# A list scheduler's model of TensorE's program loading, and the ranks of a dozen groups of work, are changed

## The chip, the cores and the metric

The kernel runs on one core of a Trainium2 chip. The metric is the device time of one execution in microseconds; the median over repeated executions counts. A profiled execution has its own time, and a span, which is the time from its first to its last instruction.

TensorE (PE) multiplies matrices, VectorE (DVE) and ScalarE (ACT) do elementwise work, SyncE (SP) and GpSimd (POOL) mostly issue transfers (DMAs).

## The reference

Two branches work on 2048 tokens of 512 channels each, and a gate per token mixes them:

```python
def _A_ref(u, ...):                       # L = 2048, D = 512, N = 128
    A = -jnp.exp(log_A_real) + 1j * A_imag
    C = (C_real + 1j * C_imag) * dt[:, None]
    P = jnp.exp((A * dt[:, None])[:, :, None] * pos[None, None, :])
    K = 2.0 * jnp.einsum("dn,dnl->dl", C, P).real
    y = irfft(rfft(u_t, 2 * L) * rfft(K, 2 * L))[:, :, :L]
    return y + u * D_skip
def _B_ref(x, w_gate, w_up, w_down):      # F = 1792
    h = einsum("bsd,df->bsf", x, w_gate) * einsum("bsd,df->bsf", x, w_up)
    return einsum("bsf,fd->bsd", h, w_down)

g = sigmoid((x * gate_w).sum(-1))
return g * a + (1 - g) * b
```

Branch B is a bilinear feed-forward layer. Branch A is a long convolution whose kernel K is made from 128 complex modes per channel, and which is done by Fourier transforms.

## The kernel before, in words

**Branch B** is most of TensorE's work. Every float32 operand is split into a high part (`hi`, rounded to the type that TensorE multiplies in one pass) and a rest (`lo`), and a product is three matmuls of 128x512: hi with lo, lo with hi, hi with hi. `pg` and `pu` are the gate and up products (operands `whi`, `wlo`, `xs`), `h` their elementwise product, which DVE makes and ACT and DVE split into `hh` and `hl`, and `y` the down product (`dhi`, `dlo`). The 1792 hidden columns are worked off in four groups of tiles, and for each group the 2048 tokens in four chunks. Finished `y` tiles are scaled into `acc` and added to the output in memory by transfers that accumulate, issued by POOL.

**Branch A** puts smaller work between these products, all of it into the PSUM tile `k`, called *sets* here: a set is a run of small matmuls that belong to one step. There are sets for the first transform of u (`k<-in,w2s` at the start), for the convolution kernel from the tables `x` and `v`, which DVE and ACT build for 32 channels at a time (`k<-v,x`), for the kernel's transform (`k<-kt,w1k_t`), the second transform (`k<-in,w2s` later on), the inverse one (`k<-y,w3s`) and the last one (`k<-in,w_t`). The `k<-v,x` and the `k<-y,w3s` sets are the dense ones: a listing of the program shows 64 matmuls for each, but every float32 matmul is run as two, so the trace shows 128, in about 2 us. Results between transforms go through memory (`su_d`, `sk_d`, `y_d`).

**The order** of all this is not written out. Every piece of work is handed to `Work.add` (line 242) as a task with its engine, an assumed duration in us, the tiles that it reads and writes, and a rank. `Work.plan` (line 340) is a list scheduler. It simulates all engines and the transfers with assumed costs, picks again and again the task that can start first (ties by rank, then by the task's number), and so fixes the order of every engine's instructions when the program is built; on the chip each engine runs its instructions in that order and waits on semaphores where it must. Three parts of this model matter here:

- `Bus` (line 170) stands for the transfers. It keeps two queues, one for those that POOL issues and one for all others, and says when each ends.
- `fetched` (line 314) stands for the loading of PE's own program. The model takes the program to come in blocks of 256 instructions, the loading of a block to be asked for `LEAD` instructions ahead of a point one block before it is needed, and to take `FETCH` us. A PE task that would run past the end of what has been loaded is planned to start later; another that can start sooner is then picked in its place.
- `EASE` (line 219) is a table of small corrections. It names groups of tasks by engine, tiles and assumed duration, and gives each a slack (it counts as ready so many us later) and a change of rank.

Of the kernel before, what the change touches and what calls it, by code (L numbers as in the profile page):

```python
# [115 lines left out]
class InOrder:  # L116


    def __init__(self, tc, engine):
        self.tc, self.engine, self.last = tc, engine, None  # L120
# [49 lines left out]
class Bus:  # L170
# [1 line left out]
    WEIGHT = 1.0, 1.58  # L172

    def __init__(self):
        self.now, self.queues = 0.0, ([], [])

    def serve(self, queues, now, until):
        done = []
# [8 lines left out]
                        done.append((q.pop(0)[0], now))  # L187
        return done

    def add(self, task, at, us):  # L190
        at = max(at, self.now)
        self.serve(self.queues, self.now, at)
        self.now = at
        self.queues[task.engine == "pool"].append([task, us])
        return self.serve([[[*x] for x in q] for q in self.queues], at, 1e9)


class Work:
# [12 lines left out]
    OVERLAP = {"act": 0.09, "dve": 0.08}  # L211


    BLOCK, FIRST, LEAD, FETCH = 256, 193, 25, 6.5
    TABLE = 1.3
    ROOM = {"dve": 0.6, "act": 0.4}
    BEYOND = 60

    EASE = {
        "act:k/in:0.32": (0.0, 1),  # L220
        "act:t/rt:0.77": (0.0, -1),
        "dve:k/kt:0.42": (0.0, -1),
        "dve:t/e/ri:0.85": (0.0, 2),
        "pool:ts:0.95": (2, 0),
        "sp:in:0.42": (0.0, 1),
    }
    DMA_RATE = 0.33

# [10 lines left out]
    def memory(self):  # L239
        return Tile(self, None, None, None, None, None, False)  # L240

    def add(self, engine, us, fn, r=(), w=(), rank=1, after=0.0, dma=0, hold=(), rows=(), count=0, slack=0.0, table=None, urgent=False):


        task = Task(len(self.tasks), engine, us, fn, rank, after, dma)
        task.rows, task.count, task.slack, task.table, task.urgent = rows, count, slack, table, urgent
        self.tasks.append(task)
        clash = lambda p, q: p is None or q is None or p == q
        split = lambda x: x if isinstance(x, tuple) else (x, None)
        for tile, part in map(split, r):  # L250
            task.deps.update(t for p, t in tile.writers if clash(p, part))
        for tile, part in map(split, w):
            task.deps.update(t for p, t in tile.writers + tile.readers if clash(p, part))
        for tile, part in map(split, r):
            tile.readers.append((part, task))
        for tile, part in map(split, w):
            tile.writers.append((part, task))
        for tile, _ in map(split, [*r, *w, *hold]):
            if tile.pool and tile not in task.tiles:
                task.tiles.append(tile)  # L260
                tile.users.append(task)
        task.deps.discard(task)
        return task
# [47 lines left out]
                return True  # L311
        return False

    def fetched(self, task, start, past):

        if not task.count:
            return start
        n0, times = past[-1][0] if past else 0, past
        n1 = n0 + task.count
        step = task.us / task.count  # L320
        first = -(-(n0 - self.FIRST) // self.BLOCK)
        b = self.FIRST + self.BLOCK * max(first, 1)
        while b < n1 + (self.BEYOND if step < 0.05 else 0):
            asked = self.passed(past, b - self.BLOCK - self.LEAD, n0, start, step)
            at = step * (b - n0) if b <= n1 else task.us + 0.11 * (b - n1)
            if asked < start:
                start = max(start, asked + self.FETCH - at)
            b += self.BLOCK
        return start

# [9 lines left out]
    def plan(self):  # L340
        for t in self.tasks:
            tags = "/".join(dict.fromkeys(tile.tag for tile in t.tiles))
            slack, rank = self.EASE.get(f"{t.engine}:{tags[:24]}:{t.us:.4g}", (0.0, 0))
            t.slack, t.rank = t.slack + slack, t.rank + rank
        left = len(self.tasks)
        free = {t.engine: 0.0 for t in self.tasks}
        order, known, rows, past, loaded = [], {}, {}, [], "exp"
        bus, then, users, need = Bus(), {}, {}, {}
        for t in self.tasks:
            need[t] = len(t.deps)  # L350
            for d in t.deps:
                users.setdefault(d, []).append(t)
                if d.dma:
                    then.setdefault(d, []).append(t)
        ready = [t for t in self.tasks if not need[t]]
        while left:
            best, wanted, found, soon = None, {}, [], {}
            for t in ready:
                at = known.get(t)
                if at is None:  # L360
                    at = known[t] = self.inputs(t)
                place = self.slots(t, at)
                found.append((t, place))
                if place is not None:
                    if t.urgent:
                        soon[t.engine] = min(place, soon.get(t.engine, 1e9))
                loose = [x for x in t.tiles if x.loose and x.made is None]
                if loose and not self.kept_waiting(t):
                    for tile in loose:
                        wanted.setdefault(tile.key, []).append((t.rank, at))  # L370
            for t, at in found:
                if at is None:
                    continue
                start = max(at, free[t.engine])
                if best and start > best[0][0]:
                    continue
                if t.rows:
                    start = max([start] + [rows[r] for r in t.rows if r in rows])
                if t.count:
                    start = self.fetched(t, start, past)  # L380
                if any(
                    rank < t.rank and when <= start
                    for tile in t.tiles if tile.made is None and tile.loose for rank, when in wanted.get(tile.key, ())
                ):
                    continue
                if not t.urgent and start < soon.get(t.engine, 0.0) < start + t.us - self.ROOM.get(t.engine, 9.0):
                    continue
                key = (start, t.rank, t.n)
                if best is None or key < best[0]:
                    best = (key, t)  # L390
            assert best, "no work can start"
            (start, _, _), t = best
            ready.remove(t)
            left -= 1
            for x in users.get(t, ()):
                need[x] -= 1
                if not need[x]:
                    ready.append(x)
            if t.count:
                past.append(((past[-1][0] if past else 0) + t.count, start, t.us, t.count))  # L400
            if t.table:
                t.us += self.TABLE * (t.table != loaded)
                loaded = t.table
            t.start, t.end = start, start + t.us
            free[t.engine] = t.end - self.OVERLAP.get(t.engine, 0.0)
            if t.dma:
                for d, end in bus.add(t, start + self.SENT[t.engine], t.dma / self.DMA_RATE / 1000):
                    d.end = end + self.LANDED[d.engine]
                    for x in then.get(d, ()):
                        known.pop(x, None)  # L410
            rows.update((r, t.end) for r in t.rows)
            for tile in t.tiles:
                if tile.made is None:
                    tile.made = start
                    tile.had.append(tile)
            order.append(t)
        return order
# [7 lines left out]
def gated_mix_kernel(  # L425
# [74 lines left out]
    def power_sets():  # L500
        for k in range(NP):
            pool_q.memset(turns[:, k : k + 1], float(TURNS[k]))

    add("dve", 0.5, memsets, w=[m_const, m_skip], rank=0)
    add("pool", 4.0, power_sets, w=[m_powers], rank=0)


    raws = {}

    def load(key, src, rank=0):  # L510
        if key in raws:
            return
        t = raws[key] = new("glu", "raw", [P, D], bufs=2)
        add("sp", 0.42, lambda: sp.dma_start(t.t, src), w=[t], dma=256, rank=rank)
# [1031 lines left out]
```

## Time and profile before

| | us |
|---|---|
| three executions | 589.75, 591.22, 588.7 (median 589.75) |
| profiled execution | 588.13 |
| its span | 586.0 |
| PE busy in it | 574.0 |
| DVE busy in it | 511.6 |
| ACT busy in it | 400.4 |
| POOL busy in it | 113.0 |

A matmul in these profiles is shown from its start to a modelled end, and the next one starts before that, so the busy time of a group is more than what it occupies; how long a run of matmuls takes is read from starts. "PEld" is the loading of a matmul's stationary operand. In a list of waits, "issue" stands for time in which an engine was idle and waited for nothing that the profile shows. The granted clock of TensorE is given as a share of full speed.

### The profile page before, as it was taken

The numbers are of one execution on the slowest core, as the hardware profiler recorded it, in microseconds if no ns is written. First come the engines' busy times: TensorE is split into PE (matmuls) and PEld (weight loads), VectorE is DVE, ScalarE is ACT, GpSimd is POOL, SyncE is SP. The second block draws the span as 40 slices with busy tenths as digits, with TensorE's granted clock in tenths as the row PEclk, the third lists the DMA queues.
The fourth block names the chain that finished last, engine by engine and source line by source line (L and its number), as shares of the span: only waits on it lengthen the run. The fifth ranks groups of instructions, "written<-read, shape, count | busy, mean of one in ns | idle before, by whom it ended". The sixth has DMA issues, their size and how long they took to land.

```text
span 586.0 us, 14846 instructions
## 1 busy us (share of the span) xinstructions
PE 574.0 (98%) x5996; PEld 434.1 (74%) x5996; DVE 511.6 (87%) x812; ACT 400.4 (68%) x891; POOL 113.0 (19%) x159
## 2 busy tenths in 40 slices
PE   8999999999999999989999999999999999999995
PEld 5777777888886767868767878876877788677763
DVE  6999999979999999996999999994999997346845
ACT  5459888897578599837897684799858743333341
POOL 0003222312010241210222301122321003112011
PEclk9999999999999999998999999999999999999998
DMA  8999969998475898987879958889968377799687
GB/s 279 400 354 365 391 223 342 274 228 262 86 190 126 282 239 177 218 231 236 178 246 237 232 152 273 196 206 206 249 181 244 89 231 138 257 333 226 204 182 138
DMA packets 71687, 136.28 MB, mean 233 GB/s; under 512 B 6852, under 2 KB 35780, under 8 KB 69188
## 3 DMA queue, kind: packets, MB, share of 16 engines
q1 hardware_dynamic: 47668, 87.10, 43.4%
q0 software_dynamic: 23392, 47.98, 39.5%
q8 instruction: 47, 0.77, 0.6%
q10 hardware_dynamic: 560, 0.26, 0.2%
q14 instruction: 20, 0.16, 0.1%
HBM read 80.27 MB, written 55.05 MB: 231 GB/s over the span
## 4 chain that ended last, share of the span: by engine, by line
PE 94%; DMA 3%; DVE 1%; issue 1%; ACT 0%; DVEq 0%; SPq 0%; ACTq 0%
PE y L124 26%; PE pg L124 26%; PE pu L124 25%; PE k L124 16%; DMA kt<-in_wts 2%; DMA ev<-in_wts 1%; DVE y L124 0%; DVE hl L124 0%; ACT dhi L124 0%; DVE h L124 0%; DVE x L124 0%; DVE dlo L124 0%; ACT h L124 0%; ACT hh L124 0%; DVE kt L124 0%
## 5 line engine op out<-in xcount | busy, mean ns | idle before, releaser
L124 PE MATMUL pg<-xs,whi 128*128 128x512 f32 x448 | 139.4, 392 | 0.4 <-ACT whi L124 0.4
L124 PE MATMUL pu<-xs,whi 128*128 128x512 f32 x448 | 138.7, 391 | 0.0
L124 PEld LDWEIGHTS pg<-xs,whi 128*128 128x128 f32 x448 | 84.5, 189 | 19.2 <-ACT whi L124 1.9
L124 PEld LDWEIGHTS pu<-xs,whi 128*128 128x128 f32 x448 | 84.6, 189 | 17.1
L124 PE MATMUL y<-dhi,hl 128*128 128x512 f32 x224 | 89.7, 400 | 1.0 <-DVE hl L124 1.0
L124 PE MATMUL pg<-xs,wlo 128*128 128x512 f32 x224 | 90.2, 403 | 0.1
L124 PE MATMUL pu<-xs,wlo 128*128 128x512 f32 x224 | 90.0, 402 | 0.0
L124 PE MATMUL y<-dlo,hh 128*128 128x512 f32 x224 | 87.4, 390 | 0.0
L124 PE MATMUL y<-dhi,hh 128*128 128x512 f32 x224 | 87.3, 390 | 0.0
L124 POOL DMA_DIRECT2D out<-acc x44 | 38.5, 968 | 178.0 <-ACT acc L124 153.3
L124 ACT COPY ev<-k 128x512 f32<-128x512 f32 x112 | 59.1, 597 | 17.1 <-PE k L124 17.0
L124 ACT CAST hh<-h 128x512 fp32r<-128x512 f32 x56 | 34.7, 619 | 43.4 <-DVE h L124 42.9
L124 ACT ACTIVATE acc<-y,ngate 128x512 f32<-128x512 f32 x62 | 41.9, 685 | 28.7 <-PE y L124 26.5
L124 DVE TENSOR_TENSOR h<-pu,h 128x512 f32<-128x512 f32 x56 | 38.5, 687 | 24.3 <-PE pu L124 23.1
L124 PEld LDWEIGHTS pg<-xs,wlo 128*128 128x128 f32 x224 | 42.2, 188 | 21.1 <-issue 11.1
L124 PEld LDWEIGHTS y<-dhi,hl 128*128 128x128 f32 x224 | 42.0, 188 | 20.2 <-issue 8.1
L124 PEld LDWEIGHTS pu<-xs,wlo 128*128 128x128 f32 x224 | 42.3, 189 | 17.9 <-issue 8.9
L124 ACT COPY h<-pg 128x512 f32<-128x512 f32 x56 | 32.8, 586 | 26.9 <-PE pg L124 21.2
L124 PEld LDWEIGHTS y<-dhi,hh 128*128 128x128 f32 x224 | 42.1, 188 | 9.0
L124 PEld LDWEIGHTS y<-dlo,hh 128*128 128x128 f32 x224 | 42.1, 188 | 8.0
L124 DVE TENSOR_TENSOR hl<-h,hh 128x512 fp32r<-128x512 f32 x56 | 38.4, 686 | 3.1 <-ACT hh L124 2.7
L124 DVE TENSOR_TENSOR x<-m,x 128x896 f32<-128x896 f32 x32 | 34.5, 1085 | 0.0
(130 smaller groups left out, 959.2 us busy)
## 6 DMA issues: line engine op xcount, KB each, us to landing
xs<-xs_d SPq DMA_DIRECT2D x36, 512.0 KB, 6.4
out<-acc POOLq DMA_DIRECT2D x44, 256.0 KB, 5.5
raw<-in_wts SPq DMA_DIRECT2D x33, 256.0 KB, 4.5
xs_d<-xs SPq DMA_DIRECT2D x16, 512.0 KB, 7.3
su_d<-ev POOLq DMA_DIRECT2D x32, 256.0 KB, 6.5
y_d<-ts SPq DMA_DIRECT2D x28, 256.0 KB, 5.9
in<-su_d POOLq DMA_DIRECT2D x12, 512.0 KB, 6.9
sk_d<-ev SPq DMA_DIRECT2D x6, 1024.0 KB, 5.8
```

The source lines that it names most:

```text
L124: got = getattr(self.engine, name)(*args, **kw)
```

## The change

In the model of the transfers, `Bus` now keeps a record of how many us of transfers were queued at each moment (`load`). In the model of program loading, the block is taken to be asked for 64 instead of 25 instructions ahead of the point, and to take 5.0 us, plus 1.05 us for each us of transfers queued 1.2 us after the asking (5 us of them at most), in place of a flat 6.5 us. So the model lets PE run a dense set across the end of a block sooner than before where little is queued (5.0 us), and later where much is (up to 10.25 us).

In `EASE`, twelve entries stand where six stood, and each has a third number, which moves the task in the tie-break by so many places. The groups are, in this order: two ACT copies out of `k` (the last quarter's kernel transform, with a slack of 3 us, and the last transform), the copy of C into `x`, the cast of weights into `whi`, the absolute value in the phases, a small DVE fix-up on the second transform (slack 3), the DVE sums into `kt`, the DVE products in the table `v`, the accumulating output of `ts`, the loads of `in` on SP, the store of `ri`, and the load of three constants at the start. The entry of the DVE products into `ri` is gone. The rest of the diff saves time while the program is built (`sign`, `place`, `seen`) and changes nothing in the order.

```diff
@@ class Bus
-        self.now, self.queues = 0.0, ([], [])
+        self.now, self.queues, self.loads = 0.0, ([], []), [(0.0, 0.0)]
...
+    def load(self, at):
+        for then, us in reversed(self.loads):
+            if then <= at:
+                return max(0.0, us - at + then)
+        return 0.0
+
     def add(self, task, at, us):
...
         self.queues[task.engine == "pool"].append([task, us])
+        self.loads.append((at, sum(x[1] for q in self.queues for x in q)))
@@ class Work
-    BLOCK, FIRST, LEAD, FETCH = 256, 193, 25, 6.5
+    BLOCK, FIRST, LEAD, FETCH = 256, 193, 64, 5.0
...
+    BEHIND = 1.05
...
-        "act:t/rt:0.77": (0.0, -1),
+        "act:t/rt:0.77": (0.0, 0, -200),
...
@@ def fetched
             if asked < start:
-                start = max(start, asked + self.FETCH - at)
+                late = self.FETCH + self.BEHIND * min(bus.load(asked + 1.2), 5.0)
+                start = max(start, asked + late - at)
@@ def plan
-            slack, rank = self.EASE.get(f"{t.engine}:{tags[:24]}:{t.us:.4g}", (0.0, 0))
-            t.slack, t.rank = t.slack + slack, t.rank + rank
+            slack, rank, late = self.EASE.get(f"{t.engine}:{tags[:24]}:{t.us:.4g}", (0.0, 0, 0))
+            t.slack, t.rank, t.late = t.slack + slack, t.rank + rank, t.late + late
...
-                key = (start, t.rank, t.n)
+                key = (start, t.rank, t.n + t.late)
```

The built programs hold the same instructions of TensorE in another order: the same 62 sets between the same products. The first place that the prediction speaks of lies at 250 to 263 us of the profile before. Between a `k<-v,x` set and the `k<-y,w3s` set after it PE had nine gate and up products:

```order
L124 MATMUL k<-v,x 32x64 x64
L124 MATMUL pg<-xs,wlo 128x512
L124 MATMUL pg<-xs,whi 128x512 x2
...
L124 MATMUL k<-y,w3s 64x128 x64
```

Now the `k<-v,x` set stands eight products later, and between the two there are eight gate and up products and three down products (33 matmuls where 27 stood):

```order
L124 MATMUL k<-v,x 32x64 x64
L124 MATMUL pg<-xs,wlo 128x512
L124 MATMUL pg<-xs,whi 128x512 x2
...
L124 MATMUL y<-dhi,hl 128x512
L124 MATMUL y<-dlo,hh 128x512
L124 MATMUL y<-dhi,hh 128x512
L124 MATMUL k<-y,w3s 64x128 x64
```

What moved is the pair of dense sets against the products around it: the first one later in the program, the second further behind it.

On SP at about the same place the loads of the next chunk's tokens (`xs`) and the stores of the inverse transform (`y_d`) stand in another order; here the difference, with what stood before marked by a minus:

```order
 L124 DMA in<-y_d 64x2048 x2
+L124 DMA xs<-xs_d 128x1024 x4
 L124 DMA w3s<-in_w 128x512 x2
-L124 DMA y_d<-ts 64x8x128 x2
-L124 DMA xs<-xs_d 128x1024
-L124 DMA y_d<-ts 64x8x128
-L124 DMA xs<-xs_d 128x1024 x2
-L124 DMA y_d<-ts 64x8x128
-L124 DMA xs<-xs_d 128x1024
+L124 DMA y_d<-ts 64x8x128 x4
```

Four loads of `xs` now go ahead of the constants `w3s` and of all four stores of `y_d`.

The last place lies at about 460 us. A `k<-v,x` set, a `k<-y,w3s` set and a `k<-in,w2s` set, which stood as `k<-y,w3s`, `k<-in,w2s`, `k<-v,x`, now follow each other with four products between each two; the first half of it on PE:

```order
L124 MATMUL k<-v,x 32x64 x64
L124 MATMUL pg<-xs,wlo 128x512
L124 MATMUL pg<-xs,whi 128x512 x2
L124 MATMUL pg<-xs,wlo 128x512
L124 MATMUL pg<-xs,whi 128x512 x2
L124 MATMUL pg<-xs,wlo 128x512
L124 MATMUL pg<-xs,whi 128x512 x2
L124 MATMUL pg<-xs,wlo 128x512
L124 MATMUL pg<-xs,whi 128x512 x2
L124 MATMUL k<-y,w3s 64x128 x64
```

The inverse transform's set has moved from ahead of the `k<-v,x` set to behind it, with twelve matmuls between.

More of the change, by code (lines that the diff above doesn't have):

```diff
@@ L217 @@
     BEYOND = 60
+    BEHIND = 1.05
     EASE = {
-        "act:k/in:0.32": (0.0, 1),
-        "act:t/rt:0.77": (0.0, -1),
[L222 to L225, printed above, removed]
+        "act:k/e:0.4": (3, 0, 0),
+        "act:k/in:0.32": (0.0, 1, 0),
+        "act:pb/x:0.31": (0.0, 0, -60),
+        "act:raw/whi:0.62": (0.0, 0, -60),
+        "act:t/rt:0.77": (0.0, 0, -200),
+        "dve:ev/y:0.6": (3, 0, 0),
+        "dve:k/kt:0.42": (0.0, -1, 0),
+        "dve:m/v:1.09": (0.0, 0, -20),
+        "pool:ts:0.95": (2, 0, 0),
+        "sp:in:0.42": (0.0, 1, 0),
+        "sp:ri:0.42": (2, 0, 0),
+        "sp:w3s/w2s/v:1.3": (0.0, 1, 0),
     }
@@ L240, in memory, with add @@
         return Tile(self, None, None, None, None, None, False)
-    def add(self, engine, us, fn, r=(), w=(), rank=1, after=0.0, dma=0, hold=(), rows=(), count=0, slack=0.0, table=None, urgent=False):
+    def add(self, engine, us, fn, r=(), w=(), rank=1, after=0.0, dma=0, hold=(), rows=(), count=0, slack=0.0, table=None, urgent=False, late=0):
         task = Task(len(self.tasks), engine, us, fn, rank, after, dma)
-        task.rows, task.count, task.slack, task.table, task.urgent = rows, count, slack, table, urgent
+        task.rows, task.count, task.slack, task.table, task.urgent, task.late = rows, count, slack, table, urgent, late
         self.tasks.append(task)
@@ L312, in kept_waiting, with fetched @@
         return False
-    def fetched(self, task, start, past):
+    def fetched(self, task, start, past, bus):
         if not task.count:
@@ L354, in plan @@
                     then.setdefault(d, []).append(t)
+            t.keys = {tile.key for tile in t.tiles}
+            t.sign = t.place = None
+        seen = {k: 0 for t in self.tasks for k in t.keys}
         ready = [t for t in self.tasks if not need[t]]
@@ L361, in plan @@
                     at = known[t] = self.inputs(t)
-                place = self.slots(t, at)
+                sign = at, sum(seen[k] for k in t.keys)
+                if t.sign != sign:
+                    t.sign, t.place = sign, self.slots(t, at)
+                place = t.place
                 found.append((t, place))
@@ L379, in plan @@
                 if t.count:
-                    start = self.fetched(t, start, past)
+                    start = self.fetched(t, start, past, bus)
                 if any(
@@ L410, in plan @@
                         known.pop(x, None)
+                    for tile in d.tiles:
+                        seen[tile.key] += 1
+            for tile in t.tiles:
+                seen[tile.key] += 1
             rows.update((r, t.end) for r in t.rows)
```

## The prediction, made before the changed kernel was run

> **What bounds the kernel now.** I read the page first, then who waited for whom on PE, then the chain of waits around the longest wait, then busy time and clock by stretch. From the page:
>
> ```profile
> span 586.0 us, 14846 instructions
> PE 574.0 (98%) x5996; PEld 434.1 (74%) x5996; DVE 511.6 (87%) x812; ACT 400.4 (68%) x891; POOL 113.0 (19%) x159
> q8 instruction: 47, 0.77, 0.6%
> ```
>
> PE is busy for 98% of the span. The third line is the queue that brings program code to PE: 47 packets, 0.77 MB, so 16.4 KB each. PE runs 5996 matmuls and as many loads, 11992 instructions, 255 for each packet: one packet is one block of the planner's 256.
>
> The list of waits, PE's rows, longest first (total, times, longest):
>
> ```profile
> PE k L124 <- issue: 2.8, 1, 2.8
> PE k L124 <- DVE acc L124: 1.5, 1, 1.5
> PE y L124 <- DVE hl L124: 1.0, 1, 1.0
> PE pg L124 <- ACT whi L124: 0.4, 1, 0.4
> ```
>
> In 586 us PE waits four times. Three of these are in the first 27 us. The longest one names no engine; this is its place in the timeline and in the chain of waits:
>
> ```profile
> 249.94 2.00 PE L124 MATMUL k<-v,x 128*32 128x64 f32 x128
> 258.21 1.98 PE L124 MATMUL k<-y,w3s 32*64 32x128 f32 x117
> 263.00 0.46 PE L124 MATMUL k<-y,w3s 32*64 32x128 f32 x11 [2.81 <-issue]
> ```
>
> PE stops inside a set, after 117 of its 128 matmuls, where no operand can be new. Busy time by stretch from the start (PE and PEld with counts), and the code queue's row in two windows, 0 to 260.1 us and 260.6 to 261.6 us:
>
> ```profile
> 0.00:260.10 260.10, 257.20 (x2374) 196.23 (x2374) 246.38 (x410) 198.82 (x438) 51.57 (x95) 1.00 0.87 260
> q8 instruction: 17, 0.28, 0.4%
> q8 instruction: 1, 0.02, 5.9%
> ```
>
> By then PE had run 4748 instructions, and some 50 semaphore instructions that the columns leave out (an estimate, from the program's count of 125 for all). 17 packets hold 4352, so about 448 were there from the start, and the 18th packet passes while PE stands still. So instruction 448 + 256 n needs the packet after n of them. Counted so in the listed order, this crossing falls on matmul 118 of the set; the timeline breaks between 117 and 118. The wait is for code.
>
> **The price of this wait** is more than its 2.81 us:
>
> ```profile
> 263.00:268.00 5.00, 5.00 (x24) 3.89 (x25) 2.78 (x3) 3.48 (x7) 0.00 (x0) 0.66 0.49 139
> 268.00:273.00 5.00, 5.00 (x23) 4.10 (x23) 2.72 (x5) 2.92 (x5) 0.00 (x0) 1.00 0.86 253
> 25.60:26.50 0.90, 0.00 (x1) 0.00 (x0) 0.90 (x4) 0.00 (x0) 0.00 (x0) 1.00 1.00 410
> 26.50:32.00 5.50, 5.44 (x24) 4.52 (x25) 5.46 (x12) 3.35 (x7) 0.00 (x0) 1.00 1.01 325
> ```
>
> The number before the last two is the granted clock: 0.66 for the 5 us after the wait, 5.00 x 0.34 = 1.7 us lost; the chain's rows bear it out:
>
> ```profile
> 254.88 2.72 PE pu L124 x12
> 263.46 3.18 PE pg L124 x9
> 266.64 3.44 PE pu L124 x12
> ```
>
> Twelve matmuls took 2.72 us before (0.227 each) and 3.44 after. 9 and 12 at 0.227 are 4.8 us, they took 6.6, and some 0.2 to 0.3 of that is the usual step out of a set. I take 1.6: the wait costs 2.8 + 1.6 = **4.4 us**. The 1.0 us wait at 25.6 us, last two of the four rows, left the clock at 1.00: a short wait costs itself alone. [...]
>
> **The change part by part.** *It removes and adds no work*: the listed order has the same 62 sets and the same products, 5996 matmuls. At 0.227 us a matmul and 0.2 for each way out of a set, PE's own time is the same. What can change is the four waits, the tail, and new waits.
>
> *The wait at 260 us.* The model now asks 39 instructions earlier and adds queued transfers. In the new order the `k<-v,x` set comes eight products later and 33 matmuls follow it, not 27; the crossing falls on matmul 88 of the `k<-y,w3s` set. From the first set's start to the crossing it was 10.1 us (249.94 to 260.1) and is 1.92 + 0.2 + 33 x 0.227 + 0.1 + 87/128 x 2.03 = 11.1. The code came 263.0 - 249.94 = 13.1 us after the first set's start. If it kept that distance, a wait of 2.0 us would remain. But in the new order PE enters the block before (one block, 256 instructions, ahead of the crossing) only at the end of the `k<-v,x` set, about 5.5 us later against the transfers that held the packet up, which are gone by then. I take 0 left, 2.0 as the other end.
>
> *New crossings.* The order puts four crossings into the second of two close sets, each with the entry into the block before inside the first: 5.5, 5.4, 4.7 and 5.2 us from entry to crossing (at about 220, 330, 462 and 468 us). For the third: entry at matmul 50 of `k<-v,x`, crossing at 38 of `k<-y,w3s`: 78/128 x 1.92 + 0.2 + 12 x 0.227 + 37/128 x 2.03 = 4.7. The nearest case before, from the timeline, and the code queue in 446.7 to 447.8 us, and the other queue in 444 to 446.7:
>
> ```profile
> 444.04 2.00 PE L124 MATMUL k<-v,x 128*32 128x64 f32 x128
> 449.59 1.14 PE L124 MATMUL k<-in,w2s 32*32 32x512 f32 x32
> 450.66 0.50 PE L124 MATMUL y<-dhi,hl 128*128 128x512 f32 x1
> q8 instruction: 1, 0.02, 5.8%
> q1 hardware_dynamic: 295, 1.06, 96.3%
> ```
>
> Entry at matmul 48 of the first, 444.76, crossing at the last matmul of the second, 450.6: 5.9 us, passed without a wait. The packet was through by 447.8, 3.0 us after the entry, though the other queue had been full till 446.7. From a packet's end to running code took 263.0 - 261.6 = 1.4 us, so the code was there 4.4 us after the entry. The four new ones have 4.7 to 5.5: they pass, by 0.3 to 1.1 us, if the packet is as quick as here. If it were as late as at 260 us (entry, in PE's sequencer some 35 instructions ahead, at about 252; code at 263: 11 us), each would cost 5.5 to 6.3 us and the clock. I take the value near the first, since the planner puts them where little is queued: 0.3 us for all four, 0 and 6 as ends.
>
> *The cover of DVE.* The twelve `EASE` entries permute DVE's and ACT's work. Rows: DVE's longest wait in 263 to 300 us, and two stretches (DVE is the third number with a count behind it, after PE and PEld):
>
> ```profile
> DVE h L124 <- PE pu L124: 4.4, 1, 4.4
> 300.00:350.00 50.00, 50.00 (x685) 37.79 (x683) 48.51 (x70) 39.05 (x96) 13.13 (x14) 1.00 0.87 219
> 350.00:400.00 50.00, 50.00 (x604) 39.96 (x600) 49.45 (x72) 38.71 (x93) 9.53 (x10) 1.00 0.88 216
> ```
>
> DVE lost 4.4 us because PE was late, so without the wait both move up together. But DVE is at 98.0 of 100 us from 300 to 400: the cover is 2 us. The reordered sums and table products are the same instructions; I cost them 0, at most 2.4 us (4.4 - 2.0) if DVE is what holds PE after that.
>
> *Start and tail.* Two loads of `dhi` go ahead of three constants, and DVE's order up to 25 us shifts by one or two instructions. The wait for `hl` stays, since the work just ahead of it is the same: 0, within 0.5. At the end:
>
> ```profile
> 573.31 6.37 PE y L124 x27
> 579.70 0.48 DVE kt L124
> ```
>
> PE ends at 579.7 and 6.3 us of DVE and output transfers follow, with the same last instructions: 0, within 0.5.
>
> *Sum.* -4.4 + 0.3 = -4.1 us in the profiled execution: span 581.9 from 586.0, and 584.0 from 588.13, of which 2.1 lie outside the span. The median is 1.6 above the profiled time, and I take the difference over: 589.75 - 4.1 = **585.6 us**.
>
> **The rivals.**
>
> *The wait moves.* Two of the four short crossings come 1 to 1.5 us late each, without loss of clock: -4.4 + 2.5 = -1.9, 587.9. For it: 0.3 us to spare at the tightest. Against: 444 us passed with a full queue.
>
> *The wait stays where it was.* Only 1.0 of 2.8 us is gained there and the clock may still fall: 589.75 - 1.0 = 588.8, or 587.1 with full clock. For it: four `xs` loads follow there sooner than they did. Against: the later entry.
>
> *DVE holds PE* from 300 us: 589.75 - 2.0 = 587.8. For it 98.0 of 100; against: PE waits for DVE nowhere past 27 us.
>
> *The wait isn't one for a packet that could be earlier*, and the order leaves it as it is: PE holds blocks far ahead, something else stops it, 589.75. Against: packet 18 lies in the idle time. [...]
>
> *Slower.* The two crossings at 462 and 468 us come one behind the other, about where POOL issues a transfer of 512 KB (the rows are from the timeline and from the list of issues, with its 6.2 us to landing):
>
> ```profile
> 473.19 0.93 POOL L124 DMA_DIRECT2D x<-su_d  x1 [18.24 <-PE k L124]
> x<-su_d POOLq DMA_DIRECT2D x2, 512.0 KB, 6.2
> ```
>
> If the packets meet it as the one at 252 us met its transfers, both crossings wait over 2.8 us and lose the clock: 2 x 4.4 - 4.4 = +4.4, 594.2. It decides (592.7) from packets that end about 5.2 us after the entry instead of 3.0: two waits of 2 us, each with 1.6 us of clock. Against: at 444 us a full queue did not do that.
>
> **How the numbers follow.** Forecast 0.50 (584.3 to 586.7); the wait moves 0.22; stays 0.09; DVE 0.06; no effect 0.05; slower 0.08. Half a percent, about what a measurement of this kernel tells from no change, is 2.9 us: 586.8 and 592.7. The forecast, and with short lateness a quarter of the second and third cases (0.08), lie below: faster 0.58. Slower 0.08. The rest, 0.34, is the same. The range 583.8 to 590.3 leaves out the slower case, the far end of the second, and a gain larger than one wait, which the executions 588.7 to 591.2 allow if they hold more than one.
>
> **What would show it.** Right: PE has no wait for "issue" over 0.5 us, the granted clock is 1.00 from 263 us to the end, PE still ends 6.3 us before the span does, span 581.4 to 582.6. Wrong: an idle time in a set at about 257 us (stays), at 220, 330 or 460 to 470 us (moves), or `k` and `y` waiting for DVE after 300 us. If the span falls by 2.8 us and the clock still dips, the clock's price was taken wrongly.

## The result, and the profile after

The changed kernel takes 585.71 us in the median of 14 runs (584.38 to 589.44), the kernel before 589.61 in 14 runs beside it (586.63 to 591.66): a ratio of 0.9944, with an interval from 0.9924 to 0.9964. It is 3.9 us faster, and 585.6 was forecast. The profiled execution was the slowest of the 14, 589.44 us, with a span of 587.5, so its profile shows where time went and not the gain; a second profile of the same kernel (`again`, below) has 583.2. Three executions among all the runs told of here were far slower than the rest (811, 948 and 3238 us) and stand in no figure.

From the page of the changed kernel, and its list of waits, PE's rows (total, times, longest):

```profile
span 587.5 us, 14848 instructions
PE 576.0 (98%) x5996; PEld 435.4 (74%) x5996; DVE 511.7 (87%) x812; ACT 399.1 (68%) x891; POOL 113.3 (19%) x159
```

```profile
PE k L124 <- issue: 1.8, 1, 1.8
PE k L124 <- DVE acc L124: 1.5, 1, 1.5
PE k L124 <- DMA in<-sk_d: 1.2, 1, 1.2
PE y L124 <- DVE hl L124: 0.6, 1, 0.6
PE pg L124 <- ACT whi L124: 0.5, 1, 0.5
```

The longest wait is again "issue", but shorter and elsewhere. The timeline shows it in a `k<-v,x` set at 130.6 us, and the set at the old place in one piece:

```profile
128.62 1.98 PE L124 MATMUL k<-v,x 128*32 128x64 f32 x125
132.36 0.30 PE L124 MATMUL k<-v,x 128*32 128x64 f32 x3 [1.76 <-issue]
...
260.92 1.99 PE L124 MATMUL k<-v,x 128*32 128x64 f32 x128
...
270.54 2.10 PE L124 MATMUL k<-y,w3s 32*64 32x128 f32 x128
```

Busy time by stretch, for the two stretches behind the new wait and the two in which DVE was the cover (the granted clock is the number before the last two):

```profile
131.00:136.00 5.00, 3.64 (x13) 2.88 (x14) 3.26 (x5) 3.38 (x10) 0.00 (x0) 0.77 0.60 124
136.00:141.00 5.00, 5.00 (x21) 4.02 (x21) 3.76 (x5) 2.86 (x5) 0.85 (x1) 0.89 0.33 93
300.00:350.00 50.00, 48.84 (x671) 36.91 (x649) 47.17 (x71) 37.96 (x94) 13.96 (x14) 1.00 0.84 205
350.00:400.00 50.00, 50.00 (x626) 39.19 (x626) 49.34 (x73) 37.34 (x92) 9.57 (x10) 1.00 0.92 238
```

The clock's price is there too: 5.00 x (0.23 + 0.11) = 1.7 us. PE lost the 1.16 us between 300 and 350 us to the one wait for `in<-sk_d`, which the kernel before had not. No wait of PE's after the first 29 us was ended by DVE.

Why was this execution 1.5 us longer than the profiled one of before, when the kernel is faster? The same 5 us near the start, the kernel before first and the changed kernel second:

```profile
5.00:10.00 5.00, 4.62 (x19) 3.39 (x19) 4.56 (x14) 3.61 (x9) 0.00 (x0) 1.00 1.06 357
```

```profile
5.00:10.00 5.00, 4.49 (x11) 3.40 (x11) 4.45 (x14) 3.48 (x8) 0.00 (x0) 1.00 1.04 340
```

PE ran 19 matmuls there in the one and 11 in the other, in the same order. (The clock column says 1.00 in both; the clock's record in the trace begins only at 5.1 us in the one and at 10.8 in the other. From one start to the next a wide matmul took 0.43 us up to 10.6 us in the changed kernel, and 0.23 from 6.7 us on in the kernel before.) The first product with `hl` started at 22.72 and 24.88 us: 2.2 us that belong to the execution and not to the kernel, as the next section shows. The rest, all in us, is -2.8 and -1.7 at 260 us, +1.8 and +1.7 at 131, +1.2 for `in<-sk_d`, -0.4 of the wait for `hl`, -0.4 after PE's end (6.0 us against 6.3): +1.6 with the 2.2, and 1.5 is measured.

### The profile page after: what moved, and what is told of

Same layout as the page of the kernel before. It is cut to its first block, busy times and chain, and to the rows that moved or that the text cites. A ratio compares the mean times of both kernels' runs of the same rounds, so it can differ in the third digit from the quotient of the medians.

```text
span 587.5 us, 14848 instructions
## 1 busy us (share of the span) xinstructions
PE 576.0 (98%) x5996; PEld 435.4 (74%) x5996; DVE 511.7 (87%) x812; ACT 399.1 (68%) x891; POOL 113.3 (19%) x159
## 4 chain that ended last, share of the span: by engine, by line
PE 91%; issue 4%; DMA 2%; POOL 1%; ACT 1%; DVE 1%; DVEq 0%; POOLq 0%; ACTq 0%
PE pg L124 26%; PE pu L124 26%; PE y L124 24%; PE k L124 15%; DMA in<-sk_d 1%; DMA y<-in_xT 1%; DMA sk_d<-ev 1%; POOL out L124 1%; POOL in L124 0%; ACT ev L124 0%; DVE y L124 0%; ACT h L124 0%; ACT xs L124 0%; DVE hl L124 0%; DVE dlo L124 0%
## 5 line engine op out<-in xcount | busy, mean ns | idle before, releaser
L124 PE MATMUL pu<-xs,whi 128*128 128x512 f32 x448 | 140.3, 395 | 0.0
L124 PEld LDWEIGHTS k<-v,x 128*32 128x32 f32 x2048 | 29.4, 110 | 7.6 <-issue 7.2
```

The source lines that it names most:

```text
L124: got = getattr(self.engine, name)(*args, **kw)
```

## The experiments

### Both kernels again

The two kernels unchanged, in the order before, changed.

> The kernel before, profiled a second time. Theory A (each execution has a code packet that comes late by chance, at a crossing that differs from run to run): PE again has one or two waits for issue inside a set, 1.5 to 4 us in all, but not surely at 260 us, and the break falls on the matmul that the count 448 + 256 n gives; the time against itself is within 0.5%. Rival (the wait at 260 us belongs to this order): a wait of 2.5 to 3.1 us after matmul 117 or 118 of the same set, and nowhere else.

> The changed kernel, profiled a second time. Its first profile has a span of 587.5 us with a wait for code of 1.8 us at 130.6 us and one of 1.2 us for a transfer. Theory A (late packets by chance): the second profile has at most one wait for code, not at the same place, and a span of 582.5 to 585. Rival (the wait at 130.6 us belongs to the new order): it is there again with 1.5 to 2 us, span 585 to 588. Ratio to the kernel before 0.992 to 0.997 either way.

The kernel before took 590.2 us, a ratio to the other runs of the same kernel of 1.0019 (1.0002 to 1.0035), which says what such a ratio is worth. The changed one took 585.01, ratio 0.9939 (0.9915 to 0.9963). In the second profile of before PE stopped in the same set after the same 117 matmuls, for 3.1 us, and the clock fell again; its first `hl` product came at 24.49 us, so the late start is no mark of the change. In the second profile of the changed kernel:

```profile
span 583.2 us, 14848 instructions
```

```profile
PE k L124 <- DMA in<-sk_d: 1.3, 1, 1.3
PE k L124 <- issue: 1.1, 1, 1.1
PE y L124 <- DVE hl L124: 0.6, 1, 0.6
```

The wait in the `k<-v,x` set came again, after the same 125 matmuls, and the one for `in<-sk_d` too. So these waits belong to the order and are no chance of one execution; only their size varies: the place is the rival's, and the span of 583.2 us lies where theory A had it, since the wait was shorter than the rival's 1.5 to 2 us and no half clock followed. This profile started as early as that of before (22.72), so the two can be compared: -2.8 and -1.7 at 260 us, +1.1 at 128, +1.3 for `in<-sk_d`, -0.4 for `hl`, -0.5 after PE's end, -3.0 us in all; the spans differ by 2.8.

### The model alone, the ranks alone

```diff
 model_only: the changed kernel with
-        (the twelve EASE entries)
+        (the six of before)
 ease_only: the changed kernel with
-    BLOCK, FIRST, LEAD, FETCH = 256, 193, 64, 5.0
+    BLOCK, FIRST, LEAD, FETCH = 256, 193, 25, 6.5
-    BEHIND = 1.05
+    BEHIND = 0.0
```

> The new model of program loading and transfers with the old table of corrections. If the model makes the gain: ratio 0.992 to 0.997, like the whole change. If the ranks make it: 0.998 to 1.002. In both, breaks inside sets fall only where the count 448 + 256 n gives them.

> The new table of corrections with the old model of program loading (25 instructions ahead, 6.5 us flat). If the ranks make the gain: ratio 0.992 to 0.997. If the model makes it: 0.998 to 1.003, with waits for code of 2 us and more where two dense sets are close.

The model alone: 584.0 us, ratio 0.9922 (0.9893 to 0.9952). The ranks alone: 588.46, ratio 0.9992 (0.9975 to 1.0009). The model makes the whole gain; the ranks by themselves give nothing that can be measured. All breaks for code in both fall where the count 448 + 256 n gives them (each page has 47 packets of the code queue, 0.77 MB, for 5996 matmuls and as many loads: 255 for a packet). But the gain is not for the reason that I had: the ranks alone do remove most of the wait at 260 us (0.6 us is left, and no half clock), and lose what that gave at the end. How long each goes on after PE's last matmul, from the chain of waits; the ranks alone first, the model alone second:

```profile
571.89 1.10 PE k L124 x16
...
576.23 2.01 DVE x L124 x5
578.24 2.91 DVE kt L124 x7
```

```profile
572.64 5.75 PE y L124 x24
578.40 0.02 issue
578.42 0.48 DVE kt L124
```

With the ranks alone the last `k<-x,w_t` set runs so late that only 12 wide matmuls (128x512; the expectations call each of them a product) follow; the chain leaves PE after it, and DVE works till 581.1 on what is made from it. With the model alone 45 follow, and DVE only has the last `y` left:

| kernel | wide matmuls after the last set | from PE's end to the span's, us |
|---|---|---|
| before (two profiles) | 27 | 6.3, 6.6 |
| changed (two profiles) | 24 | 6.0, 5.9 |
| model alone | 45 | 3.7 |
| ranks alone | 12 | 9.8 |

The model alone also has two code waits of 1.3 us (in the `k<-v,x` set at 128 us and after 126 matmuls of the `k<-y,w3s` set at 259) and no wait for `in<-sk_d`. The ranks alone have none either, so that wait comes only where the two are together. In the profile of the model alone the 4.5 us of the old wait and its clock are gone, 2.6 come back in the two code waits, and 2.6 are gained after PE's end: so the place of the last set is worth more to it than what it saves in waits. (With -0.4 for `hl` this makes -4.9, and the spans differ by 3.9; the rest I can't place.)

### The last set held back

```diff
 the model alone, with a slack for PE's task of the last k<-x,w_t set
+  slack=8.0 if q == KT - 1 and tuple(gs) == (LAST // 2,) else 0.0
```

> The kernel with the new model and the old ranks, with one edit: the last set k<-x,w_t is held back 8 us in the plan, so 12 products follow it and not 45; nothing else moves on PE. A: the time from PE's end to the span's end is set by how many products follow that set (27, 24, 45 and 12 products went with 6.3, 6.0, 3.7 and 9.8 us). Then it grows from 3.7 to 9 to 10.5 us and the time to 589 to 591 from 584.0: the whole gain is gone with PE's waits unchanged. Rival: the tail comes from the order of DVE's or the outputs' work, and stays under 5.5 us; the time stays at 584 to 586.

PE's order differs from the model alone in that one place. The time was 588.93 us, ratio 0.9996 (0.9971 to 1.0021): the gain is gone. From the chain of waits:

```profile
573.54 1.10 PE k L124 x16
...
575.07 2.02 DVE x L124 x5
577.09 2.92 DVE kt L124 x7
```

After PE's end it went on for 7.9 us in place of 3.7: less than the 9 to 10.5 that I expected, but the cause holds. PE's waits were not unchanged, as I had expected: one code wait of 0.7 us stood in place of the two of 1.3, so they don't explain the loss, they hide some of it. The place of this one set, which nobody chose, is worth as much as the whole change. The number of matmuls behind the set doesn't give the time after PE's end by itself: 12 went with 9.8 us in one kernel and with 7.9 in the other.

### The crossings moved by count alone

```diff
 the kernel before, in warm()
-            for _ in range(2):
-                pe.matmul(scratch.t, zero.t[:, :P], zero.t, ...)
+            for _ in range(17):
+                pe.matmul(scratch.t[:, :60], zero.t[:, :P], zero.t[:, :60], ...)
```

> The kernel before with its two 512-wide warm-up matmuls cut into 17 of 60 columns: 60 more PE instructions in the first 5 us, where PE waits for operands anyway, and not one moved after them. A: the wait at 260 us is for the block that begins at instruction 448 + 256 n. Then the same set breaks 30 matmuls earlier, after 87 of 128 and not after 117, with a wait of 2.8 to 3.6 us (the packet is held up by the same transfers, the need is 0.5 us earlier). Rival: the place in the program or the transfers alone stop PE, then the break stays after 117. The shift also makes two new short crossings at about 218 and 462 us, 5.0 and 5.1 us from entry to crossing, like the four of the changed kernel: A and the prediction's price for them say no wait over 0.5 us there; if they cost, a wait of 1 to 3 us each. Time 589 to 590.5.

PE's order is that of before, and every end of a block lies 60 instructions earlier in it. Both of my expectations missed. The set at the old place ran through, without a break at 87 or at 117; and one of the two new short crossings, counted on the first wide matmul behind a `k<-v,x` set, stopped PE for 3.1 us: it came 1.8 us after its entry, not the 5.0 that I had reckoned. A third short crossing, which I had not listed, stopped PE among wide matmuls at 156 us for 0.8 us. From the list of waits and the timeline, and the code queue's row in the windows 228.1 to 229.1 and 264.0 to 265.0 us:

```profile
PE pg L124 <- issue: 3.1, 1, 3.1
PE pu L124 <- issue: 0.8, 1, 0.8
```

```profile
225.53 1.99 PE L124 MATMUL k<-v,x 128*32 128x64 f32 x128
230.67 0.39 PE L124 MATMUL pg<-xs,wlo 128*128 128x512 f32 x1 [3.14 <-issue]
...
259.70 1.99 PE L124 MATMUL k<-v,x 128*32 128x64 f32 x128
...
267.96 2.10 PE L124 MATMUL k<-y,w3s 32*64 32x128 f32 x128
```

```profile
q8 instruction: 1, 0.02, 5.5%
q8 instruction: 1, 0.02, 5.9%
```

That the waits stand where the count puts them after the shift shows that they are for code. That the one went at the old place shows what decides. I had moved only the crossing in my head; its entry, 256 instructions ahead, moves with it. In the kernel before the crossing stands on matmul 118 of the second set: 117 matmuls and loads are 234 instructions, and 11 of the 27 wide matmuls between the sets make up the 256. So PE enters the block at 255.56 and wants to leave it at 259.81, 4.2 us later. Shifted by 60, all 27 lie inside: 7.9 us. Entries and crossings of these, counted in the traces, with the end of the packet (us; "at the crossing" is the start of the last instruction ahead of it):

| profile | entry | at the crossing | packet's end, after the entry | PE goes on, after the packet |
|---|---|---|---|---|
| before, 260 | 255.56 | 259.81 | 261.58, 6.0 | 263.00, 1.4 |
| shifted, 156 | 152.21 | 155.77 | 155.58, 3.4 | 156.96, 1.4 |
| shifted, 227 | 225.53 | 227.31 | 229.04, 3.5 | 230.67, 1.6 |
| shifted, 269 | 261.29 | 269.13 | 264.96, 3.7 | no wait |
| changed, 130 | 127.62 | 130.32 | 130.74, 3.1 | 132.36, 1.6 |
| changed, 272 | 262.63 | 271.80 | 267.98, 5.3 | no wait |

In the four rows with a wait PE went on 1.4 to 1.6 us after the packet's end; in the two without it came to the crossing 4.2 and 3.8 us after it. In all the profiles 15 such waits of 0.3 us or more ended 1.3 to 1.6 us after their packet. The bounds are not sharp: in the model alone a crossing among wide matmuls at 232.2 us, if the count is right there to the instruction, passed 0.9 us after its packet. What differs between the rows is the distance from entry to crossing (1.8 to 9.2 us) more than the packet's delay (3.1 to 6.0). The time was 596.15 us, ratio 1.0126 (1.0091 to 1.0162), well over the 589 to 590.5 that I expected: the 17 small matmuls took 7.5 us where two large ones took 3.8, and the start is 4.5 us longer. The two code waits and the half clock behind the longer one (5.6 us) cost more than the wait and the half clock that went (4.5).

### What holds the packet up

```diff
 the kernel before, with
 light_y:   in<-y_d carries t.t[half::2, :4] in place of t.t[half::2]
 light_lo:  the accumulation into dlo, wlo carries lo.t[:, :P] in place of lo.t
 light_both: both
```

> The kernel before with the loads in<-y_d cut to a quarter of their columns (PE reads that quarter four times over, so the last mixing step is not computed in full; nothing is moved). Two of them, 512 KB each, are issued at 254.8 us, shortly before the late packet. Theory: queued transfers make the packet late, these two most. Then the wait at 260 us falls from 2.8 or 3.1 us to under 1.0, and the time by 2 to 4.4 us. Rival: the dlo accumulations hold it, or the packet is late by itself: the wait stays at 2.5 to 3.3 us.

> The kernel before with POOL's accumulating transfers into the low parts of the weights (dlo, wlo) cut to a quarter of their columns, so three quarters of those low parts are wrong; nothing is moved. Two of them are issued at 249.5 and 255.1 us. Theory that these transfers hold the packet: the wait at 260 us falls under 1.0 us. Rival, that in<-y_d holds it: the wait stays at 2.5 to 3.3 us and the time within 0.3% of the kernel before.

> The kernel before with both cuts at once: in<-y_d and the accumulations into dlo and wlo carry a quarter of their columns (the last mixing step and the low parts of the weights are not computed in full). Alone, the first left 1.8 us and the second 2.6 us of the 3.2 to 3.5 us between the two matmuls around the wait at 260 us. Theory (the packet waits behind transfers, whose bytes add up): both leave 0.8 to 1.4 us. Rival (what is left is the packet's own way and no transfer shortens it further): 1.6 us or more, as with the first alone.

The wait in the `k<-y,w3s` set at 260 us, from one profile of each: 2.8 and 3.1 us before, 1.4 with the loads from `y_d` cut, 2.3 with the accumulations cut, 0.9 with both; the packet's end came 6.0 and 6.4, 4.6, 5.5 and 4.1 us after the entry. With both, from the list of waits:

```profile
PE k L124 <- issue: 0.9, 1, 0.9
```

So queued transfers did make this packet late, those loads most, and both cuts together did more than either, as the theory had it; but each alone does less than I expected, and 4.1 us are left with both. The accumulations' share is little more than the 0.4 us by which the two profiles of before differ. Times: 587.96 (ratio 0.9989, 0.9966 to 1.0011), 587.66 (0.9979, 0.9957 to 1.0001), 585.08 (0.9939, 0.9911 to 0.9968). With the loads cut the time fell by 0.9 us only, where I expected 2 to 4.4: PE's end came 1.9 us sooner in the profile, with no half clock, but 7.2 us followed it in place of 6.3. With both, no half clock and 0.9 us of wait left, the time fell by 3.6 us. These kernels move less data in other places too, so none of this is a clean measure of the wait's price.

### A version that follows from these readings

The entry `act:k/e` is taken out of the changed kernel's ranks, which lets 36 wide matmuls follow the last set in place of 24; and, in the second kernel, PE's warm-up gets 20 instructions more, so that the crossing at 128 us lies 10 matmuls earlier in its set and its entry 10 wide matmuls earlier.

```diff
 one_off: the changed kernel without
-        "act:k/e:0.4": (3, 0, 0),
 one_off_shift: the same, and in warm()
+            for _ in range(5):
+                pe.matmul(scratch.t[:32, :32], zero.t[:32, :32], zero.t[:32, :32], ...)
```

> The changed kernel without one of its ranks, act:k/e. In the built order 36 products follow the last set k<-x,w_t and not 24; the code crossings before 320 us stay where they were. A (the place of that set sets the time after PE's end: 27, 24, 45 and 12 products with 6.3, 6.0, 3.7 and 7.9 to 9.8 us): that time falls from 6.0 to about 4.7 us and the kernel to 583 to 584.5, the wait at 128 us stays at 1 to 2 us. Rival: the ranks are worth their place, and the kernel loses 1 us or more against the changed kernel's 585.0 to 585.7.

> The same, with five 32x32 matmuls more in PE's warm-up (20 instructions, under 1 us, before PE waits for operands in any case). No set moves; the crossing at 128 us comes 10 matmuls earlier in its set, and PE enters the block before some 2 us sooner: 4.8 us from entry to crossing in place of 2.7. A (a crossing passes if it comes later after its entry than the packet and 1.4 us): the wait of 1.1 to 1.8 us at 128 us goes, no new one over 0.5 us, and the time falls by 1 to 3 us against the one without the shift, to 581 to 583.5. Rival: the wait stays or turns up at another crossing; no gain.

Without the rank: 584.12 us, ratio 0.9916 (0.9886 to 0.9946), which the interval does not tell from the changed kernel's; its profile shows 3.9 us after PE's end in place of 6.0, with the wait in the `k<-v,x` set (1.1) and that for `in<-sk_d` (1.2) still there. With the shift: 581.29 us (581.02 to 581.56 in 6 runs), ratio 0.9863 (0.9829 to 0.9897), faster than both kernels. Its page and its list of waits, and its set at 126 us in one piece:

```profile
span 579.3 us, 14869 instructions
```

```profile
PE k L124 <- DVE acc L124: 1.5, 1, 1.5
PE y L124 <- DVE hl L124: 0.6, 1, 0.6
PE k L124 <- PE pg L124: 0.2, 1, 0.2
```

```profile
126.44 1.99 PE L124 MATMUL k<-v,x 128*32 128x64 f32 x128
```

There is no code wait left. The crossing came 4.6 us after its entry (123.40 to 127.99) in place of 2.7, and the packet had passed at 124.06. Against the one without the shift the spans differ by 2.7: 1.3 for that wait and 1.2 for `in<-sk_d`, which went too. The load that PE waited for was issued 12.2 us after the `k<-in,w2s` set before it in place of 13.0; why, with no transfer moved in the order, I haven't settled.

## Why the prediction was right, and where not, step by step

**The wait at 260 us is one for code: right.** The break came after 117 matmuls in both profiles of before, it went and others came as the count has it in the shifted kernel, and it shrank with the transfers. The rival that PE holds blocks far ahead and is stopped by something else falls.

**Its price of 4.4 us: right here, but no property of a wait.** Four waits were followed by half clock: 2.8 and 3.1 us in the kernel before, 3.1 in the shifted one and 1.8 in the changed one. The 2.3 us with the accumulations cut were not. Here are 3.41 us of both, the kernel before first, the one with the cut second; the first stretch begins 1.5 us after the wait's end, the second 1.1 us before it:

```profile
264.54:267.95 3.41, 3.41 (x10) 2.64 (x9) 1.24 (x2) 2.37 (x6) 0.00 (x0) 0.50 0.67 194
```

```profile
262.85:266.26 3.41, 2.27 (x19) 1.80 (x20) 3.41 (x5) 1.79 (x4) 0.00 (x0) 1.00 0.24 73
```

What tells them apart is in the last section.

**The wait goes to 0: right, for a reason that was not mine.** The prediction said that PE enters the block later and that "the transfers that held the packet up" are gone by then. By the packet's delay they were not: it came 5.3 us after the entry (4.9 in the second profile), hardly sooner than the 6.0 before. It compared distances from the first set's start, 10.1 to 11.1 us, which tells little; what went with the waits in the table is the distance from the entry to the crossing, and it went from 4.2 to 9.2 us, because 33 wide matmuls lie in it where 11 did. By the first reckoning 2.0 us of wait would have remained if the code were as late, by the second none; my value was the right end of the range for want of the right quantity. The figure of 11 us from the entry to code was wrong in the same way: it put the asking some 35 instructions ahead of PE, at 252 us, and against the entry itself it was 7.4. One packet of the kernel before did begin 35 instructions ahead of its entry (at 381.03 us, the entry at 382.92), but this one began 5.1 us behind it.

**The four new short crossings cost 0.3 together: right, they cost nothing.** At 232, 344, 476 and 481 us in the profile the crossing came 5.2, 5.4, 4.7 and 4.6 us after its entry, and the packets had passed 3.6, 2.4, 1.8 and 2.4 us after it. With 1.6 more this leaves nothing to spare at the first. The nearest case before was read as too roomy: the last matmul of that set started at 450.14 us, so it was 5.4 us from entry to crossing and not 5.9. That changes nothing in the sum, which went by the packet's 4.4 us. The rival on the slow side, two late packets at 462 and 468 us, did not come.

**The list of crossings was short by one.** I looked for crossings in the second of two close sets. At 130 us one set is enough: the entry lies four wide matmuls ahead of a `k<-v,x` set and the crossing behind its 125th matmul, 2.7 us later. In the kernel before it was 4.0 us there, and passed with at most 0.3 us of wait. This cost 1.1 to 1.8 us, and the clock in one profile. So the rival "the wait moves" was half true: a smaller wait, at a place that it did not name. By the signs that the prediction gave, the profiles are not those of a forecast that came out whole: "issue" is over 0.5 us in both, the clock fell in one, though not behind 263 us, and the spans, 587.5 and 583.2, lie over 581.4 to 582.6.

**DVE and ACT permuted, 0: right in that PE waited for neither after the first 29 us.** What the ranks did cost, added to the model, was in rows that I had not weighed: 1.2 us for `in<-sk_d`, and the place of the last set.

**The start and the tail.** In the two profiles with the same start, the tail was shorter by 0.5 and the wait for `hl` by 0.4, the edges of what I gave. That the tail was nearly unchanged is chance: the model alone shortens it by 2.6 us and the ranks alone lengthen it by 3.5.

**The sum.** -4.1 us was forecast for the profiled execution, -2.8 was measured between the profiles that can be compared: the -4.5 at 260 us are there, and 1.1 and 1.3 us that I had not listed were paid back, against 0.9 gained at the ends. The medians differ by 3.9. That the median fits to 0.1 us owes something to taking over the 1.6 us between profile and median; what the runs lose beside their profile varies, so the number fits better than its terms.

## What to carry to other kernels

Where an engine stops inside or near a set of short instructions and the profile names no operand, count its instructions against the packets of its code queue. What went with a wait here was the distance in time from entering a block to leaving it, against how late the packet was, and not the place of the set: the same set stopped PE with 4.2 us of distance and the packet 6.0 us after the entry, and ran through with 7.9 and 3.7. Five small matmuls in a stretch where PE waits anyway changed such a distance from 2.7 to 4.6 us without touching the order; but every crossing moves with them, so each has to be counted anew (the shift by 60 took the wait at one place away and brought 3.1 us at another). And a list scheduler's change is to be judged at the end of the program too: the place of one late set was worth as much here (588.93 us in place of 584.0) as the wait that the change was made around.

## What the runs showed of the hardware that I had not expected

**The half clock came in stretches of 3.41 us, on one grid.** In the clock's record in the trace of the kernel before, 259.41 us at full clock, 3.41 at half and 314.03 at full follow each other, then half clock to the end; in that of the changed kernel 122.88, 3.41 and 447.15. That is 76, 1 and 92 times 3.413 us in the one and 36, 1 and 131 times in the other; only the last stretch, with the end of the record, is no whole multiple. With the profile divided into stretches of 3.413 us on that grid and the waits for code laid over them, PE's idle time inside one such stretch, from the start of the last small instruction ahead of the wait, was 1.9, 2.5, 3.1 and 2.0 us where the next stretch ran at half clock, and at most 1.6 where it did not; the 2.6 us between the matmuls around the longest wait without a dip fell across two stretches, 1.5 and 1.1. So in these profiles the half clock went with the idle time inside one stretch, and not with the length of the wait. At the end of the program the half clock began 2.3 us after PE's end in the first profile of the kernel before and 2.7 us after it in that of the changed one, each time with a new stretch of the grid; in the model alone, with 3.7 us after PE's end, the mean granted clock was 1.000, so it had next to none.

**How far ahead a code packet comes varies.** In the shifted kernel and the one before, the transfers around the two sets lie at the same times after the first set's start: loads `in<-y_d` are issued 4.9 us after it in both. With the entry 1.6 us after it the packet passed at 4.3 to 5.3, with the entry at 5.6 it passed at 10.7 to 11.6, behind those loads. My estimate from these times, if the queue treats both alike: the request in the kernel before came after the gap that the other packet used, less than 1.3 us ahead of the entry. No row shows the request itself. In a stretch of long matmuls of the changed kernel a packet passed at 454.89 to 456.46 us, with the entry at 459.36: it ended 2.9 us ahead of it, where the one at 260 us before ended 6.0 behind. I can't say what sets the lead.

**The version without code waits hardly scatters.** Its 6 runs lie within 0.5 us, against 5.0 us for 14 runs of the kernel before and 5.1 for the changed one. Six runs of the changed kernel (`again`) lie within 1.9 us, so the number of runs makes some of this. The varying length of the code waits and of the clock behind them would do the rest, but the start must have been steadier too, since it alone differed by 2.2 us between profiles of kernels with the old warm-up; no run tests either alone.
